# Another order of the loading phase, and of batch 4's input, in a block of two cross attentions and a gated feed-forward

## The chip, the cores and the metric

The kernel runs on one core of one Trainium2 chip. The metric is the time of one execution in microseconds (us). Engines are named as the profile names them: PE is TensorE (matrix products; PEld its weight loads), DVE is VectorE, ACT is ScalarE, POOL is GpSimd, and SP is SyncE, which here only issues transfers.

## The reference

There are 8 batches of 8 heads. x has 512 rows of 64 per head, the state 32 rows of 64. Two softmax attentions cross x and the state, and a gated feed-forward follows.

```python
scores = scale * np.matmul(x, state.transpose(0, 1, 3, 2))       # 512 x 32 per head
a = softmax(scores);   xread = np.matmul(a, state)
scores2 = scale * np.matmul(state, x.transpose(0, 1, 3, 2))      # 32 x 512 per head
a2 = softmax(scores2); sread = np.matmul(a2, x)
y = np.concatenate([xread, sread], axis=2)                       # heads side by side: (8*544, 512)
out = (1/(1+np.exp(-(y @ w_gate))) * (y @ w_val)) @ w_out        # 512 -> 1536 -> 512
```

## The kernel before

The rows of xread of one batch are worked on together, 512 at a time; the rows of sread of all batches form a last group, which the code calls batch 8 (B). The feed-forward of batches 0 and 1 is mixed into the loading phase, and batches 2 to 8 follow in a loop.

Because xread is attention times state, the kernel never forms it. It multiplies the state with the gate and value weights first (SW, the "visits" at line 231: `sw_visit` in the loading phase, `sw_wide` in the loop) and the transposed attention aT with that. Per batch the work on TensorE is:

- the scores of x with the state (`S_mm`, line 121), in two halves i = 0 and 1 of four heads each; then maximum (`S_max`) and subtraction (`S_sub`) on DVE, the exponential (`S_exp`) on ACT, sum and reciprocal (`n_sum`) on DVE and the normalising product (`n_mul`, line 152) on POOL or DVE;
- the transposed attention aT: by TensorE (`aT_mm`, copied by `aT_cp`) for batches 0 and 1, by four DMA transposes on SP (`aT_dma`, line 173) for the others;
- twelve gate-and-value products `gv_mm(b, f)` (line 283), f being a block of 128 of the 1536 hidden columns; then a tanh on ACT (`gv_th`) and one operation on DVE (`gv_glu`, line 298);
- twelve groups of four products with w_out (`out_mm`, line 314), whose results leave by SP in four stores;
- the scores of the state with x (`cT_mm` to `cT_nrm`), transposed by two DMA transposes on SP (`c_dma`, line 209), and their sums over x (`sr_mm`, line 216).

x comes in by `load_x`, is cast to bf16 (`cast_x`, line 91), and transposed: by TensorE and a copy (`xT_mm`, `xT_cp`) for batches 0 and 1, and by four DMA transposes on SP (`at_xT_dma`, line 113) for the others. The state comes in through `load_s` and `load_sb`, and `sT_mm` with `sT_pad`, `sT_cp` and `pad` lay it out transposed in sTz and sTc. `load_w` and `load_wo` fetch the weights in pieces on POOL's queue. `gate` is a tiny copy on POOL that makes what POOL issues next wait for a given tile. `warm` issues products that nobody reads.

The schedule is manual: every engine runs its instructions in the order in which the program issues them, and each waits only for what it needs. Until line 690 that order is a flat list written out call by call; this is the loading phase. PSUM has two buffers for gate products (GV), four that weight visits and others share (SWP), and one each called OU and AT; a product waits until the buffer that it is given has been read. In SBUF x has three buffers in float32, xT, aT and the attention two each.

In the loop over b from 2, block f of batch b goes with `out_mm(b - 1, f)`, and the work of the next batch nb = b + 1 is spread over the f: `row` (scores to aT_dma, in six steps t), `col` (scores of the state with x, to c_dma), the weight visits at f = 0 and 6, and x of the batch after it: loaded at f = 6, cast on POOL and transposed at f = 1. For b = 2 the steps of `row` come one f later than for the other batches, and the sums over x come at f = 9 in place of f = 3.

Of the kernel before, what the change touches and what calls it, by code (L numbers as in the profile page):

```python
# [16 lines left out]
def kernel(  # L17
# [70 lines left out]
    def cast_x(b, cp, lo, n):  # L88
        if b not in xbs:
            xbs[b] = xp.tile((128, 4, H, D), BF, name="xb" if b > 1 else "xb01", bufs=3 if b > 1 else 2)  # L90
        cp(xbs[b].rearrange("p c h d -> p h c d")[:, lo:lo + n], xfs[b][:, lo:lo + n])  # L91
# [15 lines left out]
    def xT_cp(b, j, cp):  # L107
        cp(xT_tile(b)[:, j], held["xT", b, j])
# [235 lines left out]
    def warm(n, place):  # L344

        ps = place[0].tile((128, 512), FP, name="warm", tag=place[1])
        for _ in range(n):
            nc.tensor.matmul(ps[:, :128], ones[:, 0], ones[:, 0], start=True, stop=True)  # L348
# [80 lines left out]
        nc.vector.memset(ones[:, e, 64 - e * 64:128 - e * 64], 0.0)  # L429
# [2 lines left out]
    nc.vector.memset(sTz, 0.0)
# [18 lines left out]
    xT_cp(1, 1, act)
    xT_mm(1, 2, GV)
    cast_x(1, pool, 6, 2)
    cast_x(0, vec, 0, 2)
# [3 lines left out]
    xT_mm(0, 0, AT)
    xT_mm(1, 3, SWP)
    cast_x(0, act, 2, 2)  # L460
    xT_mm(0, 1, GV)
    xT_cp(0, 0, act)
    xT_cp(1, 3, act)
    warm(3, OU)
    load_w(0, 0, 256)
# [28 lines left out]
    n_sum(1, 1)
    sT_cp(1, act)
    sw_cp(0, 256, 2, 0, act)
    warm(8, GV)
    S_max(0, 0)
    sw_visit(1, 256, 256)
# [2 lines left out]
    sw_cp(1, 256, 2, 1, act)
    S_sub(0, 0)
    S_max(0, 1)
    S_exp(0, 0)
    n_mul(1, 1, nc.gpsimd)
    aT_mm(1, GV)
# [10 lines left out]
    warm(15, GV)
    load_w(1, 1024, 512)
    gate(xfs[0][:, 7, 0, 0:1])  # L520
    aT_cp(1, 1, vec)
    gv_mm(1, 3, GV)
# [23 lines left out]
    sw_visit(1, 512, 512, 0)
    sw_visit(0, 512, 512, 0)
    gv_th(1, 1)
    sw_cp(1, 512, 0, 1, act)
    gv_glu(1, 1)  # L550
    gv_mm(0, 0, GV)
    gv_th(0, 0)
    sw_cp(0, 512, 0, 0, act)
    sw_cp(0, 512, 0, 1, vec)
# [4 lines left out]
    gv_mm(1, 4, SWP)
    gv_glu(0, 0)  # L560
    gv_mm(1, 5, GV)
    gv_th(1, 5)
    cast_x(2, vec, 4, 4)
    gv_th(1, 4)
    gv_mm(0, 2, SWP)
    gv_th(0, 2)
# [1 line left out]
    gv_glu(1, 5)
    gv_mm(0, 1, GV)
    sT_cp(3, act)  # L570
    gv_glu(1, 4)
    pad(2, 6)
    gv_glu(0, 2)
    gv_mm(0, 5, SWP)
    gv_th(0, 1)
    gv_glu(0, 1)
    sw_visit(0, 1024, 512, 0)
    gv_th(0, 5)
    gv_glu(0, 5)
    sw_cp(0, 1024, 0, 0, act)  # L580
    gv_mm(1, 0, GV)
    gate(glus[1][:, 4, 0:1])
    sw_cp(0, 1024, 0, 1, vec)
    gv_mm(0, 7, SWP)
    load_wo(0)
    sw_visit(0, 1024, 512, 1)
    gv_th(1, 0)
    gv_glu(1, 0)
    gv_th(0, 7)
    gv_glu(0, 7)  # L590
    gv_mm(0, 6, GV)
    gv_mm(0, 4, SWP)
    sw_cp(0, 1024, 1, 1, act)
    sw_cp(0, 1024, 1, 0, vec)
    gv_mm(0, 10, SWP)
    gv_mm(0, 9, SWP)
    at_xT_dma(2)
    S_mm(2, 0, SWP)
    gv_mm(0, 11, GV)
    gv_th(0, 4)  # L600
    gv_mm(0, 8, SWP)
    gv_glu(0, 4)
    out_mm(0, 0, GV)
    load_wo(1)
    gv_th(0, 6)
    gv_glu(0, 6)
# [3 lines left out]
    gv_th(0, 9)  # L610
    gv_glu(0, 9)
    gv_th(0, 11)
    gv_th(0, 8)
    load_wo(2)
# [3 lines left out]
    S_mm(2, 1, GV)
    out_mm(0, 6, AT)
    load_x(3, nc.gpsimd)  # L620
    cast_x(3, pool, 4, 4)
# [45 lines left out]
    sw_cp(1, 1024, 1, 1, vec)
    sw_cp(2, 1, 0, 0, act)
    gv_mm(1, 6, GV)
    sw_cp(1, 1024, 1, 0, act)  # L670
    cT_nrm(2, 0, nc.gpsimd)
    sw_cp(2, 1, 0, 1, act)
    gv_th(1, 6)
    gv_mm(1, 9, SWP)
    gv_th(1, 9)
    at_xT_dma(3)
    gv_glu(1, 6)
    out_mm(0, 5)
    gv_glu(1, 9)
    gv_mm(1, 8, GV)  # L680
    gv_th(1, 8)
    gv_glu(1, 8)
    gv_mm(1, 10, SWP)
    gv_th(1, 10)
    gv_mm(1, 11, GV)
    gv_glu(1, 10)
    gv_th(1, 11)
# [1 line left out]
    load_x(4, nc.sync)
    gv_glu(1, 11)  # L690
# [83 lines left out]
```

## Time and profile before

| what | value |
|---|---|
| median of 3 runs | 236.31 us (235.29 to 237.57) |
| profiled execution | 237.39 us, of which 235.6 us is the span from its first to its last instruction |
| mean granted clock of TensorE | 0.993 |
| TensorE, ACT, DVE, POOL busy | 224.3, 144.0, 139.6, 68.5 us |
| read from and written to HBM | 18.35 and 8.91 MB |

In a profile an instruction's line says when it starts, how long it takes, its engine, its source line, what it writes and reads, and in brackets how long its engine stood idle before it and what ended that. The granted clock is the share of full speed that TensorE was allowed. A transfer shows up twice: as the instruction that issues it (SPq is SP's queue) and, in the list of issues, with its time from issue to landing. Times within the span count from its first instruction.

### The profile page before, as it was taken

How to read it: one execution, taken by the hardware profiler on the slowest of the kernel's cores; microseconds unless marked ns; L12 is line 12 of the kernel's file. 1: busy time of each engine (PE TensorE's matmuls, PEld its weight loads, DVE VectorE, ACT ScalarE, POOL GpSimd, SP SyncE). 2: the span in 40 equal slices, each digit the busy share in tenths (PEclk: the TensorE clock that was granted, in tenths of full speed). 3: DMA queues.
4: the chain of work that ended last, by engine and by line, in shares of the span. 5: the costliest groups of instructions: out<-in, count | busy, mean ns of one | idle time of the engine just before them, and what ended most of it. 6: DMA issues, size and time to landing. Idle time of an engine off the chain costs nothing.

```text
span 235.6 us, 4975 instructions
## 1 busy us (share of the span) xinstructions
PE 224.3 (95%) x1887; PEld 112.4 (48%) x1887; DVE 139.6 (59%) x267; ACT 144.0 (61%) x290; POOL 68.5 (29%) x74
## 2 busy tenths in 40 slices
PE   5798999999999959999999999999999999999994
PEld 4674434444444424444444444444444444566754
DVE  3599889946586526754774567556765664432211
ACT  3679777957585825848485857585748555432311
POOL 4876180062024143303520261113110426100001
PEclk9999999999999979999999999999999999999999
DMA  6999969817553458527451665214122312311104
GB/s 205 273 200 289 180 99 188 236 36 200 127 177 67 136 138 220 156 49 268 83 143 37 178 167 123 69 56 92 46 70 67 90 57 79 89 45 67 69 22 114
DMA packets 47271, 29.49 MB, mean 125 GB/s; under 512 B 29872, under 2 KB 42544, under 8 KB 47248
## 3 DMA queue, kind: packets, MB, share of 16 engines
q1 hardware_dynamic: 40096, 21.84, 34.0%
q0 software_dynamic: 6864, 7.14, 16.4%
q10 hardware_dynamic: 288, 0.20, 0.5%
q8 instruction: 15, 0.25, 0.5%
q14 instruction: 8, 0.07, 0.1%
HBM read 18.35 MB, written 8.91 MB: 116 GB/s over the span
## 4 chain that ended last, share of the span: by engine, by line
PE 79%; DVE 6%; ACT 4%; DMA 3%; SPq 3%; issue 2%; POOL 2%; ACTq 0%; DVEq 0%; POOLq 0%
PE outp L314 33%; PE gvp L283 30%; PE gvp L286 5%; PE swp L231 4%; DVE glu L298 3%; DMA xf<-in_x_dram 2%; SPq L173 2%; ACT th L293 2%; PE Sp L121 2%; PE srp L216 1%; PE warm L348 1%; DVE rs L144 1%; PE outp L334 1%; PE cTp L181 1%; DMA aT<-ab 1%
## 5 line engine op out<-in xcount | busy, mean ns | idle before, releaser
L298 DVE SCALAR_TENSOR_TENSOR glu<-th,gvp 128x512 bf16<-128x512 f32 (+1 forms) x108 | 70.2, 657 | 72.2 <-ACT th L293 52.1
L283 PE MATMUL gvp<-aT,SW 128*128 128x512 bf16 x384 | 97.5, 379 | 3.3 <-DMA aT<-ab 2.5
L314 PE MATMUL outp<-wo,glu 128*128 128x512 bf16 x396 | 100.4, 384 | 0.0
L293 ACT ACTIVATE th<-gvp 128x512 f32<-128x512 f32 (+1 forms) x108 | 61.4, 575 | 56.2 <-PE gvp L283 46.7
L283 PEld LDWEIGHTS <-SW 128*128 128x128 bf16 x384 | 36.3, 98 | 49.3 <-issue 8.9
L314 PEld LDWEIGHTS <-glu 128*128 128x128 bf16 x396 | 37.1, 98 | 41.3 <-issue 3.4
L269 ACT CAST SW<-swp 128x512 bf16<-128x512 f32 x74 | 41.1, 587 | 4.0 <-PE swp L231 2.9
L204 POOL TENSOR_SCALAR cN<-cE,rc 128x512 bf16<-128x512 f32 x16 | 25.0, 1565 | 59.1 <-DVE rc L201 57.4
L318 ACT ACTIVATE res<-outp 128x512 f32<-128x512 f32 x33 | 19.7, 597 | 17.2 <-PE outp L314 17.0
L152 POOL TENSOR_TENSOR ab<-E,ri 128x512 bf16<-128x512 f32 x14 | 14.6, 1048 | 32.1 <-ACT E L137 15.3
L91 POOL CAST xb<-xf 128x1024 bf16<-128x1024 f32 (+1 forms) x13 | 12.5, 977 | 33.1 <-DMA xf<-in_x_dram 27.8
L269 DVE CAST SW<-swp 128x512 bf16<-128x512 f32 x22 | 14.7, 681 | 3.6 <-PE swp L231 3.6
L196 ACT ACTIVATE cE<-cTp,nb 128x512 f32<-128x512 f32 x16 | 11.1, 693 | 1.2 <-POOL cN L204 1.2
L129 DVE TENSOR_REDUCE mx<-Sp 128x16 f32<-128x512 f32 x16 | 10.9, 679 | 1.1 <-PE Sp L121 1.1
L134 DVE TENSOR_TENSOR E<-Sp,mx 128x512 f32<-128x512 f32 x16 | 11.0, 686 | 0.2
L188 DVE TENSOR_REDUCE cm<-cTp 128x1 f32<-128x512 f32 x16 | 10.9, 683 | 0.0
L144 DVE TENSOR_REDUCE rs<-E 128x16 f32<-128x512 f32 x16 | 10.8, 678 | 0.1
L137 ACT ACTIVATE E<-E 128x512 f32<-128x512 f32 x16 | 10.2, 639 | 0.5 <-DVE E L134 0.5
L325 POOL DMA_DIRECT2D out_dram<-res x2 | 1.1, 554 | 29.7 <-ACT res L318 29.7
L231 PE MATMUL swp<-wg,sTc 64*32 64x512 bf16 (+1 forms) x192 | 8.4, 328 | 0.1
L121 PEld LDWEIGHTS <-xT 128*128 128x128 bf16 x128 | 6.8, 108 | 3.2 <-issue 0.8
L231 PEld LDWEIGHTS <-sTc 64*32 64x32 bf16 x384 | 4.6, 91 | 7.4 <-issue 5.1
(62 smaller groups left out, 140.3 us busy)
## 6 DMA issues: line engine op xcount, KB each, us to landing
out_dram<-res SPq DMA_DIRECT2D x31, 256.0 KB, 2.4
xf<-in_x_dram SPq DMA_DIRECT2D x12, 256.0 KB, 4.6
xf<-in_x_dram SPq DMA_DIRECT2D x3, 1024.0 KB, 6.1
wo<-in_moe_w_out_dram POOLq DMA_DIRECT2D x3, 512.0 KB, 8.0
wv<-in_moe_w_val_dram POOLq DMA_DIRECT2D x2, 512.0 KB, 10.1
wg<-in_moe_w_gate_dram POOLq DMA_DIRECT2D x2, 512.0 KB, 9.8
xf<-in_x_dram POOLq DMA_DIRECT2D x2, 512.0 KB, 7.8
xf<-in_x_dram POOLq DMA_DIRECT2D x1, 1024.0 KB, 13.4
```

Source lines behind the costliest of these rows:

```text
L91: cp(xbs[b].rearrange("p c h d -> p h c d")[:, lo:lo + n], xfs[b][:, lo:lo + n])
L144: nc.vector.tensor_reduce(rs, halfE(b, i), AX.X, ALU.add)
L152: eng.tensor_tensor(abs_[b].rearrange("p c e (j n) -> p (c e) j n", n=Ns)[:, ce, 2 * i:2 * i + 2], halfE(b, i)[:, ce], ri[:, ce].unsqueeze ...
L204: eng.tensor_scalar(held["cN", b][:, e], held["cE", b, e], rc, None, op0=ALU.mult)
L231: nc.tensor.matmul(pss[e][j * Ns:(j + 1) * Ns, o:o + n], sTc[rows, b, j] if b > 1 else sTz[rows, b, j, e], (wg, wv)[w][rows, j, lo:lo + n] ...
L269: cp(*sw_left.pop((b, lo, w, e)))
L283: nc.tensor.matmul(ps, SWs[b][:, g, w, fs], aTs[b][:, :, g], start=(g == 0), stop=(g == 1))
L286: nc.tensor.matmul(ps, (wg, wv)[w][:, j, fs], XS[:, j], start=(j == 0), stop=(j == 3))
L293: nc.scalar.activation(th, held["gv", b, f][0], AF.Tanh, scale=0.5)
L298: nc.vector.scalar_tensor_tensor(glus[b][:, f], held["th", b, f], 1.0, held["gv", b, f][1], ALU.add, ALU.mult)
L314: nc.tensor.matmul(ops[b, c], glus[b][:, f, c * 128:(c + 1) * 128], wo[:, f], start=(f == 0), stop=(f == NF - 1))
L318: nc.scalar.activation(res, ops[b, c], AF.Copy, scale=0.5)
```

## The change

The diff leaves every helper as it is. It does three things.

The flat list of the loading phase is given another order: the first list below shows its old beginning, the second its new one up to the first gate products of batch 0. Warm-up products come first (12, 16, 3 and 3 of them, then 15); the clearing of sTz moves from the head of DVE's list to behind a cast; batch 1's two halves of scores, maxima, subtractions and exponentials follow one another directly; the first quarters of the weights are loaded first, the state of batches 4 and 5 (`load_sb(2)`) later; gate products start with f = 1, 2 and 0 of batch 1, and four of them (f = 8 to 11) wait until the end of the list.

```diff
-    nc.vector.memset(sTz, 0.0)
     load_x(1, nc.sync, 4)
-    warm(16, GV)
-    nc.scalar.activation(pre[:, 0:1], ones[:, 0, 0:1], AF.Exp)
-    cast_x(1, act, 2, 2)
-    cast_s(0, pool)
-    sT_mm(0, OU)
-    sT_pad(0, 1, vec)
-    load_x(0, nc.sync, 4)
-    cast_x(1, pool, 0, 2)
-    xT_mm(1, 0, SWP)
-    xT_cp(1, 0, vec)
...
-    S_mm(1, 0, SWP)
-    xT_cp(1, 2, vec)
-    S_max(1, 0)
...
-    S_mm(1, 1, SWP)
-    S_exp(1, 0)
...
-    S_max(1, 1)
-    xT_cp(0, 2, act)
-    load_sb(3)
-    load_w(1, 0, 256)
-    warm(6, OU)
-    S_sub(1, 1)
-    load_sb(2)
-    load_w(0, 512, 512)
```

```diff
+    warm(12, SWP)
+    warm(16, GV)
+    warm(3, SWP)
     load_x(1, nc.sync, 4)
+    warm(3, AT)
     cast_x(1, pool, 0, 2)
     xT_mm(1, 0, SWP)
+    load_w(1, 0, 256)
+    warm(15, OU)
+    nc.scalar.activation(pre[:, 0:1], ones[:, 0, 0:1], AF.Exp)
+    cast_s(0, pool)
+    load_sb(1)
+    load_w(0, 0, 256)
+    cast_x(1, vec, 4, 2)
+    nc.vector.memset(sTz, 0.0)
+    sT_mm(0, SWP)
+    load_x(0, nc.sync, 4)
+    cast_x(1, act, 2, 2)
     xT_cp(1, 0, vec)
+    xT_mm(1, 2, AT)
+    xT_mm(1, 1, GV)
+    cast_x(1, act, 6, 2)
+    sT_pad(0, 1, vec)
+    load_w(0, 256, 256)
+    xT_mm(1, 3, SWP)
     load_w(1, 256, 256)
...
+    S_mm(1, 0, GV)
+    S_max(1, 0)
+    xT_cp(1, 3, act)
+    S_mm(1, 1, GV)
+    S_max(1, 1)
...
+    S_sub(1, 1)
...
     load_w(1, 512, 512)
...
     S_sub(1, 0)
+    gate(xfs[0][:, 7, 0, 0:1])
...
+    load_sb(3)
+    load_w(0, 512, 512)
     S_mm(0, 0, GV, (0,))
+    S_mm(0, 0, AT, (1,))
+    S_exp(1, 1)
+    n_sum(1, 1)
     S_exp(1, 0)
+    sw_visit(0, 0, 256)
+    n_sum(1, 0)
+    sw_visit(1, 0, 256)
...
+    n_mul(1, 1, nc.gpsimd)
+    sw_cp(1, 0, 2, 0, act)
+    S_max(0, 0)
+    S_sub(0, 0)
+    n_mul(1, 0, nc.gpsimd)
+    aT_mm(1, AT)
+    sw_visit(1, 256, 256)
     load_sb(2)
...
+    gv_mm(1, 1, GV)
+    warm(6, SWP)
...
+    gv_mm(1, 2, SWP)
...
+    sw_visit(1, 512, 512, 1)
+    gv_mm(1, 0, GV)
...
+    sw_visit(1, 512, 512, 0)
...
+    sT_mm(2, AT)
...
+    aT_mm(0, OU)
```

At the end of the list the load of x 4 moves from behind the second transposes of batch 2 to ahead of them (`at_xT_dma(3)`, `load_x(4, nc.sync)`, ..., `c_dma(2)`). The two `n_mul` of batch 2 go from DVE to POOL; of the casts of x 2 the second half goes from DVE to POOL, and of x 3 from POOL to DVE.

In the loop, batch 3 takes the form that batch 2 has (rows one f later, sums over x at f = 9), and at b = 2 the casts and transposes of x 4 move from f = 1 to f = 6, the load of x 5 from f = 6 to f = 8:

```diff
-                if f == (4 if b > 2 else 10):
+                if f == (4 if b > 3 else 10):
                     sr_cp(b, 0, act)
                     sr_cp(b, 1, vec)
-                if 0 <= f - (b == 2) < 6:
-                    row(nb, f - (b == 2))
+                if 0 <= f - (b < 4) < 6:
+                    row(nb, f - (b < 4))
                 elif f >= 7:
                     col(nb, f - 7)
-                if f == 6 and nb + 2 < B:
+                if f == (6 if b > 2 else 8) and nb + 2 < B:
                     load_x(nb + 2, nc.sync, 4 if nb + 3 == B else 1)
-                if f == 1 and nb + 1 < B:
+                if f == (1 if b > 2 else 6) and nb + 1 < B:
                     cast_x(nb + 1, pool, 0, 4)
                     cast_x(nb + 1, pool, 4, 4)
                     at_xT_dma(nb + 1)
-            if b < B and f == (3 if b > 2 else 9):
-                sr_mm(b, AT if b > 2 else SWP)
+            if b < B and f == (3 if b > 3 else 9):
+                sr_mm(b, AT if b > 3 else SWP)
```

More of the change, by code (lines that the diff above doesn't have):

```diff
@@ L451 @@
[L451 to L454, printed above, removed]
-    S_mm(1, 0, SWP)
-    xT_cp(1, 2, vec)
-    S_max(1, 0)
[L458 to L465, printed above, removed]
-    S_sub(1, 0)
-    xT_cp(0, 1, act)
-    cast_x(0, act, 4, 2)
+    xT_cp(1, 2, vec)
+    cast_x(0, vec, 0, 2)
+    cast_x(0, pool, 4, 2)
+    xT_cp(1, 1, act)
+    S_mm(1, 0, GV)
@@ L469 @@
+    S_max(1, 0)
+    xT_cp(1, 3, act)
+    S_mm(1, 1, GV)
+    S_max(1, 1)
+    cast_x(0, act, 2, 2)
+    xT_mm(0, 1, OU)
+    xT_mm(0, 2, AT)
+    xT_cp(0, 1, act)
+    S_sub(1, 1)
+    xT_mm(0, 0, OU)
+    xT_cp(0, 2, act)
+    load_w(1, 512, 512)
+    cast_x(0, pool, 6, 2)
+    S_sub(1, 0)
+    gate(xfs[0][:, 7, 0, 0:1])
+    xT_cp(0, 0, vec)
+    xT_mm(0, 3, GV)
+    warm(8, SWP)
+    load_sb(3)
+    load_w(0, 512, 512)
     S_mm(0, 0, GV, (0,))
-    S_mm(1, 1, SWP)
+    S_mm(0, 0, AT, (1,))
@@ L494 @@
[L494 to L499, printed above, removed]
+    sw_visit(0, 0, 256)
+    n_sum(1, 0)
+    sw_visit(1, 0, 256)
+    xT_cp(0, 3, act)
+    sw_cp(0, 0, 2, 1, act)
+    S_mm(0, 1, GV, (0,))
+    S_mm(0, 1, OU, (1,))
+    sw_cp(0, 0, 2, 0, act)
+    n_mul(1, 1, nc.gpsimd)
[5 more added lines that the diff above has]
+    sw_visit(1, 256, 256)
+    load_sb(2)
@@ L500 @@
+    sw_cp(1, 0, 2, 1, act)
+    aT_cp(1, 0, act)
+    S_exp(0, 0)
+    S_max(0, 1)
+    sw_visit(0, 256, 256)
+    aT_cp(1, 1, vec)
+    S_sub(0, 1)
+    sw_cp(0, 256, 2, 0, vec)
+    sT_mm(1, OU)
+    gv_mm(1, 1, GV)
+    warm(6, SWP)
+    n_sum(0, 0)
     sw_cp(1, 256, 2, 0, act)
+    sw_cp(1, 256, 2, 1, act)
+    gv_mm(1, 2, SWP)
+    S_exp(0, 1)
     sw_cp(0, 256, 2, 1, vec)
[L502 to L507, printed above, removed]
@@ L508 @@
-    aT_cp(1, 0, act)
     load_x(2, nc.gpsimd, 2)
+    gv_th(1, 1)
     sw_visit(1, 512, 512, 1)
-    S_sub(0, 1)
-    S_exp(0, 1)
+    gv_mm(1, 0, GV)
+    gv_th(1, 2)
+    gv_glu(1, 1)
+    sT_cp(1, vec)
+    sT_mm(3, OU)
+    sw_cp(1, 512, 1, 1, act)
+    n_sum(0, 1)
+    sw_visit(1, 512, 512, 0)
+    sw_cp(1, 512, 1, 0, act)
+    gv_th(1, 0)
+    sw_visit(0, 512, 512, 0)
+    sT_cp(3, act)
+    gv_glu(1, 2)
+    load_w(0, 1024, 512)
+    n_mul(0, 0, nc.gpsimd)
+    sT_mm(2, AT)
+    load_w(1, 1024, 512)
@@ L513 @@
+    sw_cp(1, 512, 0, 1, act)
+    sw_cp(0, 512, 0, 0, act)
+    n_mul(0, 1, nc.gpsimd)
+    aT_mm(0, OU)
+    sw_cp(1, 512, 0, 0, vec)
+    aT_cp(0, 0, act)
+    aT_cp(0, 1, act)
+    gv_mm(1, 6, SWP)
+    cast_x(2, pool, 0, 4)
     sw_visit(0, 512, 512, 1)
-    sw_cp(0, 512, 1, 0, act)
-    sw_cp(1, 512, 1, 1, act)
-    load_w(0, 1024, 512)
+    gv_th(1, 6)
     sw_cp(0, 512, 1, 1, act)
[L518 to L522, printed above, removed]
@@ L546 @@
[L546 to L554, printed above, removed]
+    gv_mm(1, 5, GV)
+    gv_th(1, 5)
+    sw_cp(0, 512, 0, 1, vec)
+    gv_glu(1, 0)
+    gv_mm(0, 0, SWP)
+    gv_th(0, 0)
+    gv_glu(1, 6)
+    cast_x(2, pool, 4, 4)
+    sw_cp(0, 512, 1, 0, vec)
+    gv_glu(0, 0)
+    gv_mm(0, 5, SWP)
+    gv_mm(1, 4, SWP)
+    gv_th(1, 4)
@@ new lines @@
+    gv_mm(0, 2, GV)
+    gv_th(0, 5)
+    gv_th(0, 2)
+    gv_glu(1, 5)
+    gv_mm(0, 7, SWP)
+    gv_glu(1, 4)
+    sT_cp(2, act)
+    gv_mm(0, 6, SWP)
+    gv_th(0, 7)
+    gv_glu(0, 5)
+    gv_th(0, 6)
+    gv_glu(0, 2)
+    gv_mm(1, 7, GV)
+    gv_glu(0, 7)
+    gv_th(1, 7)
+    sw_visit(0, 1024, 512, 0)
+    sw_cp(0, 1024, 0, 0, act)
+    gv_glu(0, 6)
+    sw_cp(0, 1024, 0, 1, act)
+    sw_visit(0, 1024, 512, 1)
+    gv_glu(1, 7)
+    sw_cp(0, 1024, 1, 1, act)
+    sw_cp(0, 1024, 1, 0, vec)
@@ L555 @@
+    gv_mm(0, 4, GV)
+    pad(2, 6)
+    gv_th(0, 4)
+    load_wo(0)
+    gv_mm(0, 1, SWP)
+    gv_th(0, 1)
+    gv_mm(0, 8, SWP)
+    at_xT_dma(2)
+    gv_th(0, 8)
+    gv_mm(0, 9, GV)
+    S_mm(2, 1, OU)
+    gv_glu(0, 4)
+    gv_th(0, 9)
+    load_wo(1)
+    gv_glu(0, 1)
+    gv_glu(0, 8)
+    load_wo(2)
+    gate(glus[1][:, 4, 0:1])
+    gv_glu(0, 9)
+    S_max(2, 1)
+    gv_mm(1, 3, SWP)
+    gv_th(1, 3)
     gv_mm(0, 3, SWP)
     gv_th(0, 3)
-    cast_x(2, pool, 0, 4)
-    sw_cp(1, 512, 0, 0, vec)
@@ L559 @@
[L559 to L566, printed above, removed]
-    gv_glu(0, 3)
[L568 to L606, printed above, removed]
+    gv_glu(1, 3)
+    S_sub(2, 1)
@@ L607 @@
+    load_x(3, nc.gpsimd)
+    gv_glu(0, 3)
+    gv_mm(0, 11, SWP)
+    gv_th(0, 11)
+    gv_glu(0, 11)
+    gv_mm(0, 10, GV)
     gv_th(0, 10)
@@ L609 @@
     sw_wide(2, 0)
[L610 to L614, printed above, removed]
+    S_exp(2, 1)
+    out_mm(0, 1, GV)
+    sw_cp(2, 0, 1, 0, act)
+    sw_cp(2, 0, 2, 0, act)
+    sw_cp(2, 0, 0, 1, vec)
+    n_sum(2, 1)
+    n_mul(2, 1, nc.gpsimd)
+    sw_cp(2, 0, 2, 1, act)
+    S_mm(2, 0, SWP)
     S_max(2, 0)
+    out_mm(0, 6, GV)
+    out_mm(0, 3)
     S_sub(2, 0)
     S_exp(2, 0)
[L618 to L621, printed above, removed]
@@ L667 @@
[L667 to L687, printed above, removed]
+    n_sum(2, 0)
+    out_mm(0, 7, AT)
+    sw_cp(2, 0, 1, 1, act)
@@ new lines @@
+    out_mm(0, 5)
+    n_mul(2, 0, nc.gpsimd)
+    gate(xTs[2][:, 0, 3, 0:1])
+    aT_dma(2)
+    cast_x(3, pool, 0, 4)
+    cT_mm(2, (SWP, SWP))
+    cT_max(2, 1)
+    cast_x(3, vec, 4, 4)
+    sw_visit(1, 1024, 512, 1)
+    sw_cp(1, 1024, 1, 1, act)
+    sw_cp(1, 1024, 1, 0, act)
+    out_mm(0, 8)
+    out_mm(0, 9)
+    cT_exp(2, 1)
+    sw_visit(1, 1024, 512, 0)
+    sw_cp(1, 1024, 0, 1, vec)
+    sw_cp(1, 1024, 0, 0, act)
+    out_mm(0, 0, GV)
+    sw_cp(2, 0, 0, 0, vec)
+    out_mm(0, 11)
+    gv_mm(1, 8, SWP)
@@ new lines @@
+    gv_th(1, 8)
+    cT_max(2, 0)
+    cT_exp(2, 0)
+    gv_glu(1, 8)
+    out_mm(0, 2)
+    sw_wide(2, 1)
+    sw_cp(2, 1, 0, 0, vec)
+    sw_cp(2, 1, 1, 1, vec)
+    at_xT_dma(3)
+    load_x(4, nc.sync)
+    sw_cp(2, 1, 1, 0, act)
+    sw_cp(2, 1, 0, 1, act)
+    out_mm(0, 10)
+    gv_mm(1, 9, SWP)
+    sw_cp(2, 1, 2, 0, act)
+    gv_th(1, 9)
+    gv_glu(1, 9)
+    out_mm(0, 4)
+    gv_mm(1, 11, SWP)
+    gv_th(1, 11)
+    sw_cp(2, 1, 2, 1, vec)
+    gv_glu(1, 11)
+    gv_mm(1, 10, GV)
+    gv_th(1, 10)
@@ L688 @@
+    gv_glu(1, 10)
+    cT_nrm(2, 0, nc.gpsimd)
+    cT_nrm(2, 1, nc.gpsimd)
     c_dma(2)
[L689 to L690 removed]
     for b in range(2, B + 1):
```

81 lines of the change are left out of this document (removed).

## The prediction

> **What bounds the kernel now.** I read the page first (who is busy), then busy time by stage (where TensorE stops), then the waits of TensorE, then the queues behind the longest of them.
>
> ```profile
> PE 224.3 (95%) x1887; PEld 112.4 (48%) x1887; DVE 139.6 (59%) x267; ACT 144.0 (61%) x290; POOL 68.5 (29%) x74
> ```
>
> TensorE works 95% of the span. The next view cuts the span at the weight products that open a batch; its columns are length, then busy time (and instructions) of PE, PEld, DVE, ACT and POOL, granted clock, DMA share, GB/s.
>
> ```profile
> 0.00:10.00 10.00, 5.74 (x56) 4.65 (x57) 3.84 (x11) 4.46 (x9) 6.78 (x16) 1.00 0.90 247
> 10.00:14.30 4.30, 4.30 (x51) 4.30 (x50) 3.69 (x7) 3.66 (x8) 2.29 (x4) 1.00 1.33 202
> 14.30:24.70 10.40, 9.63 (x183) 5.13 (x180) 8.99 (x18) 8.55 (x18) 7.78 (x10) 1.00 1.26 250
> 24.70:57.70 33.00, 33.00 (x260) 14.20 (x252) 25.89 (x46) 24.70 (x48) 10.30 (x12) 1.00 0.77 157
> 57.70:81.70 24.00, 23.92 (x201) 11.04 (x200) 15.67 (x29) 16.36 (x34) 4.04 (x4) 1.00 0.49 129
> 81.70:110.20 28.50, 25.86 (x209) 11.62 (x216) 15.68 (x29) 16.68 (x34) 7.77 (x7) 0.94 0.56 152
> 110.20:134.30 24.10, 23.98 (x208) 10.89 (x212) 15.59 (x29) 16.43 (x34) 7.16 (x7) 1.00 0.46 120
> 134.30:158.50 24.20, 24.08 (x209) 10.99 (x216) 15.60 (x29) 16.53 (x34) 7.26 (x7) 1.00 0.43 113
> ```
>
> From 24.7 us TensorE has no gap for 33 us, and batch after batch takes 24.0 to 24.2 us. One stage doesn't fit: the stage of batch 3 (81.7 to 110.2) takes 28.5. The waits of TensorE, and two cuts inside that stage, say why:
>
> ```profile
> PE gvp L283 <- DMA aT<-ab: 2.5, 1, 2.5
> 82.60:85.10 2.50, 0.01 (x1) 0.04 (x2) 0.25 (x2) 0.67 (x2) 2.25 (x2) 1.00 0.25 51
> 86.00:89.50 3.50, 3.50 (x17) 1.53 (x16) 1.98 (x3) 0.31 (x1) 0.00 (x0) 0.51 0.87 285
> ```
>
> The first gate product of batch 3 waits 2.5 us for the transposed attention (aT) of batch 3, and behind that stop the granted clock is 0.51 for 3.5 us, another 3.5 x 0.49 = 1.7 us. Together 4.2; the stage is 28.5 - 24.1 = 4.4 too long. I take 4.3. Why aT is late stands in the lists of POOL, DVE, SP and TensorE and in the chain:
>
> ```profile
> 63.20 0.57 SPq L74 DMA_DIRECT2D xf<-in_x_dram  x1
> 69.40 2.02 POOL L91 CAST xb<-xf 128x1024 bf16<-128x1024 f32 x2 [14.38 <-DMA xf<-in_x_dram]
> 71.39 2.06 POOL L152 TENSOR_TENSOR ab<-E,ri 128x512 bf16<-128x512 f32 x2
> 71.36 0.25 DVE L146 RECIPROCAL ri<-rs 128x16 f32<-128x16 f32 x1
> 71.45 5.13 SPq L113 DMA_TRANSPOSE xT<-xb  x4
> 77.78 6.04 SPq L173 DMA_TRANSPOSE aT<-ab  x4
> 82.58 2.38 DMA aT<-ab
> 83.93 0.52 SPq L74 DMA_DIRECT2D xf<-in_x_dram  x1
> 61.95 0.40 PE L121 MATMUL Sp<-sTz,xT 128*128 128x64 bf16 x8
> ```
>
> x of batch 4 is asked for at 63.20 and lands about 69.4. POOL's casts of it hold it to 71.4, so batch 3's normalisation (L152) ends at 73.45. SP's four transposes of x (5.13 us), then two output stores, stand ahead of aT, which starts at 77.78 although its data was there at 73.45; its last piece lands at 84.96. TensorE wanted it at about 82.5. So aT is 4.3 us late by the queue's order and 2.5 us late for its reader.
>
> **The change part by part.** *Stage of batch 2.* The casts and transposes of x of batch 4 go from f = 1 to f = 6, behind batch 3's aT; the load of x 4 goes ahead of batch 2's second transposes (c_dma), that of x 5 from f = 6 to f = 8. The last row sum of batch 3 is ready at 71.36 + 0.25 = 71.6. With no cast ahead, POOL's second product starts there and ends at 72.7 (half of 2.06 each). aT starts then, takes 6.04 with its last issue 4.8 us in (77.78 to 82.58), and lands 2.38 later: 79.9, against 82.5. The wait goes, and with it the low clock: -4.3. Bounds: none of the low clock returned, -2.5; all of the stage's excess, -4.4.
>
> The Trainium skill ("TensorE: Matmul & The Clock Gate", Part 1) has the clock fall after an idle window of about 3.4 us, free-running; by that a stop of 2.5 us need not cost clock, and the term would be -2.5 and the whole 234.9. The 0.51 row disagrees here, and the row decides.
>
> What is late next? x 4's transposes follow aT: 78.8 to 83.9, last piece landing some 2.4 us after its issue, 85.1. Batch 4's first scores now sit at f = 1 of batch 3; batch 2's stage has that form today, and there they start 61.95 - 57.7 = 4.25 into it: 85.95. Margin 0.8. The load of x 5 follows at about 84.4 (store at f = 8 between); such loads land in
>
> ```profile
> xf<-in_x_dram SPq DMA_DIRECT2D x3, 1024.0 KB, 6.1
> ```
>
> 6.1 us: 90.5. Casts 2.0 and transposes 5.1 end at 97.7, two stores 1.0, so aT of batch 4 starts at 98.7 and lands 7.2 later at 105.9; TensorE wants it at 81.7 + 24.1 + 0.8 = 106.6. Margin 0.7: I put 0.2 for this, between 0 and, if x 5 came as late in its stage as x 4 does today, the same 4.3 again. The second transposes, pushed behind x 4 and x 5, feed the sums over x (sr_mm); those of batch 3 move to f = 9 with the score rows, where batch 2's are today; no cost.
>
> *Loading phase.* The same loads, casts, copies and products in another order. Two of POOL's products of batch 2 replace DVE's, one cast of x 2 goes to POOL and one of x 3 to DVE. TensorE fills its gaps there with warm-up products, so what counts is when the in-order chain on DVE lets it go. Rows that carry the chain (DVE unless another engine is named):
>
> ```profile
> xf<-in_x_dram SPq DMA_DIRECT2D x2, 256.0 KB, 4.4
> 8.16 0.61 DVE L91 CAST xb<-xf 128x512 bf16<-128x512 f32 x1 [2.12 <-DMA xf<-in_x_dram]
> 1.24 0.91 DVE L432 MEMSET sTz<- 128x1024 uint32 x1 [0.16 <-issue]
> 5.62 0.42 DVE L108 COPY xT<-xTp 128x512 bf16<-128x512 bf16 x1 [0.62 <-PE xTp L105]
> L129 DVE TENSOR_REDUCE mx<-Sp 128x16 f32<-128x512 f32 x16 | 10.9, 679 | 1.1 <-PE Sp L121 1.1
> L134 DVE TENSOR_TENSOR E<-Sp,mx 128x512 f32<-128x512 f32 x16 | 11.0, 686 | 0.2
> L144 DVE TENSOR_REDUCE rs<-E 128x16 f32<-128x512 f32 x16 | 10.8, 678 | 0.1
> L269 ACT CAST SW<-swp 128x512 bf16<-128x512 f32 x74 | 41.1, 587 | 4.0 <-PE swp L231 2.9
> 13.73 2.05 POOL L152 TENSOR_TENSOR ab<-E,ri 128x512 bf16<-128x512 f32 x2 [1.25 <-DVE ri L146]
> 18.97 1.02 PE L283 MATMUL gvp<-aT,SW 128*128 128x512 bf16 x4
> 22.73 0.62 PE L159 MATMUL aTp<-ident,ab 128*128 128x128 bf16 x8 [0.48 <-POOL ab L152]
> ```
>
> The third part of x 1 is issued near 1.8 and lands 4.4 later: 6.2. DVE casts it (6.8), and only then clears sTz, which today is done by 2.15: 0.91 (7.7). Two copies and a pad of 0.42 (8.9), a cast (9.4). Both maxima and both subtractions of batch 1, waiting until 9.6 for scores that follow a pad and two copies on ACT (an estimate): 4 x 0.68 = 12.3. A copy, then two sums with reciprocals of 0.97: ready at 13.7 and 14.65, so POOL's two products end at 15.75. Today they end at 13.73 + 2.05 = 15.78. Taking both halves first gains nothing, because the late clear eats it. Then maximum, subtraction, maximum for batch 0 (16.7); aT's copy on DVE follows ACT's, which stands behind four weight copies (14.7 + 5 x 0.59 = 17.6), and ends at 18.0; the last subtraction frees the PSUM buffer of the first gate product's second half at 18.7. So that product is done near 19.2 (today 18.97 + 1.02 = 20.0). But DVE has weight copies, sums and glu in front of it still: 18.7 + two copies 1.3 + sum 0.95 + glu 0.65 + small copy 0.35 + sum 0.95 + glu 0.65 = 23.5, when the product of weights at line 231 gets its PSUM buffer; with it, its twin and sT, aT of batch 0 starts at 24.5, against 22.73. At 25.1 TensorE then has three gate products and seven weight visits behind it; today, at 24.7, three and eight, and a visit takes 0.4. Loss 0.8, and 0.1 for short waits on glu up to 31 us: +0.9. Bounds: the first gate product's lead, -0.8; and 24.5 - 22.73 plus two 0.4 visits out of place, +2.6.
>
> From there to the loop all gate products of batch 0 and 1 but four come before the outputs. DVE is busy 25.9 of 33.0 us there and ACT 24.7, with no stop on TensorE, and the change leaves both engines' number of instructions as it is to within two; cost 0. x 4, at present landing at 69.4, then comes near 65.
>
> Sum: -4.3 + 0.2 + 0.9 = -3.2. The profiled execution took 237.39 (span 235.6 and 1.79 around it), so 234.2; it is 1.08 above the median of the runs, 236.31, so 233.1 on the median's scale, which I forecast. A measurement of this kernel tells about 1% from no change (runs of 235.29 to 237.57), 2.4 us.
>
> **The rivals.** *The full clock comes early (232.3).* The pace of the warm-up products changes today:
>
> ```profile
> 1.02 1.89 PE L348 MATMUL warm<-ones 128*128 128x128 bf16 x16 [1.02 <-DVE ones L429]
> 13.08 1.42 PE L348 MATMUL warm<-ones 128*128 128x128 bf16 x12
> 17.85 1.01 PE L348 MATMUL warm<-ones 128*128 128x128 bf16 x15
> ```
>
> 118 ns each until 14, 67 after, and only once TensorE had been busy without a break from 10 us. After, 34 such products run back to back (34 x 0.118 = 4.0 us), so it could be fast from 5 us, and transposes, scores and visits up to 18 take half their time: the 0.8 comes back. For it: the dense start. Against: gaps between 7 and 13, and DVE, not TensorE, times this phase. That is what the skill's warm-up rule on the same page (about 3.4 us of sustained work) would make of it; the pace rows agree with it.
>
> *The wait moves to batch 4 (237.4).* Were x 5 to land 3 us later in its stage than 90.5, aT of batch 4 would miss its reader by 2.5 and the clock would fall: 233.1 + 4.3. For it: a margin of 0.7 only. Against: x 5 is now asked for 26.7 us into the stage of batch 2, three us earlier for its use than x 4 today.
>
> *The loading phase costs 1.7 more (234.8),* its upper bound: every buffer wait falls on TensorE.
>
> *Slower: the state of batches 4 and 5 comes late (239.7).* load_sb(2) moves on POOL from 10.37 to behind batch 1's products, 15.8. Its transposes stand on TensorE ahead of aT of batch 0 and everything after.
>
> ```profile
> 10.37 0.60 POOL L359 DMA_DIRECT2D sb<-in_state_dram  x1
> sb<-in_state_dram POOLq DMA_DIRECT2D x3, 64.0 KB, 8.4
> xf<-in_x_dram POOLq DMA_DIRECT2D x1, 1024.0 KB, 13.4
> ```
>
> At 8.4 it lands at 24.2, just in time for 24.3. At 13.4, POOL's slowest, it lands at 29.2: 4.9 of stop and 1.7 of clock, 233.1 + 6.6. Over 1% slower from a landing at 28.0. Against: it is small, and only weights issued before it are ahead of it.
>
> **How the numbers follow.** Forecast 0.50; early clock 0.20; loading at its bound 0.10; wait moved 0.12; late state 0.08. Faster by over 1% is below 233.9: early clock, and 0.48 of the forecast's 0.50: 0.68. Slower (over 238.7): 0.08. The rest, 0.24, is within 1%. Range: from 230.8 (the loading bound of -0.8 in place of +0.9, and 0.6 for the spread of runs) to 236.5, which leaves out the moved wait and the late state.
>
> **What would show it.** Right: no wait of L283 on aT, clock 1.0 at 80 to 90, the stage of batch 3 near 24.2 us, aT of batch 3 issued near 73 after the opening of batch 2 at about 58; aT of batch 0 near 24.5. Wrong: a stop of L283 a batch later, a wait of L369 on the state's DMA, or gaps between 25 and 57 us.

## The result and the profile after

The kernel after takes 234.56 us (median of 20 runs, 232.84 to 235.91) against 236.62 (20 runs, 234.72 to 238.33): 0.9908 of before, 95% interval 0.9884 to 0.9932. That is 2.1 us or 0.9%, a gain, but under 1%; 233.1 was forecast. The traced execution took 233.25 us with a span of 231.5. Its page, and its stages cut at the opening of each batch (the first weight product of `sw_wide`), with the columns explained ahead of the prediction's second view:

```profile
PE 221.3 (96%) x1887; PEld 110.6 (48%) x1887; DVE 138.2 (60%) x266; ACT 143.0 (62%) x288; POOL 71.6 (31%) x77
```

```profile
24.70:56.50 31.80, 31.80 (x260) 13.80 (x253) 24.20 (x41) 23.54 (x46) 9.87 (x13) 1.00 0.83 156
56.50:80.50 24.00, 23.92 (x203) 11.04 (x202) 15.83 (x31) 16.35 (x34) 7.17 (x6) 1.00 0.62 132
80.50:104.50 24.00, 23.92 (x201) 11.03 (x200) 15.60 (x29) 16.41 (x34) 7.22 (x6) 1.00 0.60 141
104.50:129.90 25.40, 24.24 (x201) 10.87 (x201) 15.59 (x29) 16.56 (x34) 7.66 (x7) 1.00 0.64 161
129.90:154.00 24.10, 23.98 (x201) 10.92 (x200) 15.58 (x29) 16.42 (x34) 7.16 (x7) 1.00 0.40 107
```

The rows are the end of the loading phase and the stages of batches 2, 3, 4 and 5. The stage of batch 3 is down from 28.4 to 24.0, with the clock at 1.00. That of batch 4, regular before, is 1.3 too long. The waits of TensorE and SP's list show why:

```profile
PE gvp L283 <- DMA aT<-ab: 0.6, 1, 0.6
PE srp L216 <- DMA Eb<-cN: 0.4, 1, 0.4
```

```profile
58.24 0.58 SPq L74 DMA_DIRECT2D xf<-in_x_dram  x1
71.67 5.04 SPq L173 DMA_TRANSPOSE aT<-ab  x4
76.81 6.46 SPq L113 DMA_TRANSPOSE xT<-xb  x4
84.01 0.39 SPq L74 DMA_DIRECT2D xf<-in_x_dram  x1
92.66 5.57 SPq L113 DMA_TRANSPOSE xT<-xb  x4
99.43 5.06 SPq L173 DMA_TRANSPOSE aT<-ab  x4
104.60 0.52 SPq L74 DMA_DIRECT2D xf<-in_x_dram  x1
106.53 3.01 SPq L209 DMA_TRANSPOSE Eb<-cN  x2
```

Read it downwards. Batch 3's aT goes out at 71.67, ahead of x 4's transposes, as the change says. Behind those, x 5 is asked for at 84.01; its transposes start at 92.66, aT of batch 4 only at 99.43, and the first gate product of batch 4 waits 0.6. x 6 then goes out at 104.60, 1.9 us ahead of the second transposes of batch 4 (Eb), for which the sums over x wait another 0.4. The stop that the change removes has come back one stage later, smaller, and without the loss of clock.

### The profile page after: what moved, and what is told of

Read it like the earlier page. It is cut to its first block, busy times and chain, and to the rows that moved or that the text cites. A ratio compares the mean times of both kernels' runs of the same rounds, so it can differ in the third digit from the quotient of the medians.

```text
span 231.5 us, 4984 instructions
## 1 busy us (share of the span) xinstructions
PE 221.3 (96%) x1887; PEld 110.6 (48%) x1887; DVE 138.2 (60%) x266; ACT 143.0 (62%) x288; POOL 71.6 (31%) x77
## 3 DMA queue, kind: packets, MB, share of 16 engines
q0 software_dynamic: 6864, 7.14, 16.7%
## 4 chain that ended last, share of the span: by engine, by line
PE 79%; DVE 7%; DMA 4%; ACT 4%; POOL 2%; issue 2%; SPq 1%; ACTq 0%; DVEq 0%; POOLq 0%
PE outp L314 33%; PE gvp L283 31%; PE gvp L286 5%; PE swp L231 4%; DVE glu L298 3%; DMA Eb<-cN 2%; DMA xf<-in_x_dram 2%; PE srp L216 2%; POOL cN L204 1%; PE cTp L181 1%; ACT th L293 1%; PE outp L334 1%; PE Sp L121 1%; DVE rs L144 1%; ACT SW L269 1%
## 5 line engine op out<-in xcount | busy, mean ns | idle before, releaser
L314 PE MATMUL outp<-wo,glu 128*128 128x512 bf16 x396 | 99.0, 379 | 0.0
L283 PE MATMUL gvp<-aT,SW 128*128 128x512 bf16 x384 | 97.4, 379 | 1.5 <-DMA aT<-ab 0.6
L283 PEld LDWEIGHTS <-SW 128*128 128x128 bf16 x384 | 36.3, 98 | 47.0 <-issue 6.2
L314 PEld LDWEIGHTS <-glu 128*128 128x128 bf16 x396 | 36.6, 98 | 40.7 <-issue 2.8
L204 POOL TENSOR_SCALAR cN<-cE,rc 128x512 bf16<-128x512 f32 x16 | 24.9, 1564 | 64.5 <-DVE rc L201 55.7
L152 POOL TENSOR_TENSOR ab<-E,ri 128x512 bf16<-128x512 f32 x16 | 16.7, 1047 | 42.5 <-DVE ri L146 34.8
L91 POOL CAST xb<-xf 128x1024 bf16<-128x1024 f32 (+1 forms) x14 | 13.6, 987 | 15.0 <-PE gvp L283 6.6
L121 PEld LDWEIGHTS <-xT 128*128 128x128 bf16 x128 | 6.0, 100 | 4.4 <-issue 1.0
```

The lines of the kernel that those rows point to most:

```text
L152: eng.tensor_tensor(abs_[b].rearrange("p c e (j n) -> p (c e) j n", n=Ns)[:, ce, 2 * i:2 * i + 2], halfE(b, i)[:, ce], ri[:, ce].unsqueeze ...
L204: eng.tensor_scalar(held["cN", b][:, e], held["cE", b, e], rc, None, op0=ALU.mult)
L283: nc.tensor.matmul(ps, SWs[b][:, g, w, fs], aTs[b][:, :, g], start=(g == 0), stop=(g == 1))
L314: nc.tensor.matmul(ops[b, c], glus[b][:, f, c * 128:(c + 1) * 128], wo[:, f], start=(f == 0), stop=(f == NF - 1))
```

## The experiments

Two theories stood against each other after the result. A, the prediction's: the stop came from the order, x 4's casts and transposes ahead of batch 3's attention. B: it came from x 4 being asked for too late, and the list's move of that load is what counts. The table gives, from each trace, the opening of batch 2 and the lengths of the stages of batches 3 and 4 (starts of the first weight products), and the ratio to before.

| kernel | opening of batch 2 | stage 3 | stage 4 | median us | ratio, 95% interval |
|---|---|---|---|---|---|
| before | 57.7 | 28.4 | 24.1 | 236.62 | 1 |
| after | 56.5 | 24.0 | 25.4 | 234.56 | 0.9908 (0.9884 to 0.9932) |
| after, second trace | 57.2 | 24.0 | 25.7 | 234.01 | 0.9891 (0.9858 to 0.9924) |
| loop alone | 57.0 | 24.0 | 25.9 | 234.11 | 0.9900 (0.9867 to 0.9932) |
| list alone | 56.5 | 24.1 | 24.1 | 232.22 | 0.9818 (0.9784 to 0.9851) |
| before, x 4 sooner | 56.3 | 24.9 | 24.1 | 232.56 | 0.9822 (0.9788 to 0.9856) |
| list alone, x 4 late | 57.0 | 29.2 | 24.1 | 237.10 | 1.0028 (0.9993 to 1.0064) |
| after, x 5 at f = 6 | 57.0 | 26.3 | 24.1 | 234.35 | 0.9889 (0.9858 to 0.9921) |
| after, x 5 at f = 3 | 56.8 | 24.0 | 24.1 | 232.18 | 0.9814 (0.9783 to 0.9845) |
| list and row shift | 56.8 | 24.0 | 24.1 | 232.30 | 0.9810 (0.9777 to 0.9844) |
| x 4 sooner and row shift | 57.1 | 24.0 | 24.1 | 232.41 | 0.9857 (0.9813 to 0.9901) |
| list alone, clear first | 56.7 | 24.3 | 24.1 | 232.30 | 0.9802 (0.9769 to 0.9834) |
| list alone, few warm-ups | 56.5 | 24.7 | 24.1 | 232.30 | 0.9822 (0.9789 to 0.9855) |

**The loop alone.** The list of before with the loop of after.

```diff
-                if f == 6 and nb + 2 < B:
+                if f == (6 if b > 2 else 8) and nb + 2 < B:
...
-                if f == 1 and nb + 1 < B:
+                if f == (1 if b > 2 else 6) and nb + 1 < B:
```

> The list of the loading phase as before, the loop as after: casts and transposes of x 4 at f = 6 of batch 2's stage, x 5 loaded at f = 8, batch 3 in batch 2's form. Theory A (the prediction's: the stop in the stage of batch 3 came from x 4's casts and transposes standing ahead of batch 3's attention): the loading phase ends at 57.7 as before, the stage of batch 3 takes 24.0 to 24.2 in place of 28.5, the stage of batch 4 about 1.3 more (x 5 late, as in the trace of after), ratio near 0.987. Theory B (the stop came from x 4 being asked for too late; the list's earlier load is what removes it): the same stage times, since this order doesn't need x 4 early. Theory C (the profiled run of before shows a longer stop than a typical one): ratio 0.992 to 0.996 although the profile shows the whole 4 us gone.

Stage 3 is whole again, stage 4 is 1.8 too long, ratio 0.990: the loop brings the change's whole gain, and its whole loss, without the new list. The ratio lies between the 0.987 of theories A and B and the 0.992 of C; the section on the prediction comes back to C.

**The list alone.** The list of after with the loop of before: x 4 is still cast at f = 1, ahead of batch 3's attention.

> The list as after, with x 4 loaded ahead of the second transposes of batch 2, the loop as before: casts and transposes of x 4 at f = 1, ahead of batch 3's attention on POOL and SP. Theory A: the order is what counts, the stop of L283 on aT in the stage of batch 3 stays (1 to 2.5 us, with a low clock behind it), ratio 0.995 to 1.004. Theory B: x 4 is asked for at 58.2, lands near 64.6, its casts end at 66.7 and its transposes on SP at 72, so aT of batch 3 starts at 72 to 73 and lands by 80, ahead of its reader at 81.3: no stop, and none in the stage of batch 4 either, since x 5 is asked for at f = 6; ratio 0.976 to 0.983, faster than the whole change.

```profile
58.04 0.58 SPq L74 DMA_DIRECT2D xf<-in_x_dram  x1
66.64 5.14 SPq L113 DMA_TRANSPOSE xT<-xb  x4
72.98 5.05 SPq L173 DMA_TRANSPOSE aT<-ab  x4
```

SP's list of this run: x 4's transposes do stand ahead of aT, and do no harm, because x 4 landed at 64.6 and they are through when the attention is ready. No wait of TensorE in stages 3 and 4, and 0.982, twice the gain of the whole change. Theory A's order is sufficient, as the loop alone showed, but not needed; B stands.

**One line.** Before, with the load of x 4 moved as in the change.

```diff
     at_xT_dma(3)
+    load_x(4, nc.sync)
     gv_glu(1, 6)
...
     c_dma(2)
-    load_x(4, nc.sync)
```

> The kernel before with one line moved: x 4 is loaded behind the transposes of x 3 and ahead of the second transposes of batch 2. Theory A: the casts and transposes of x 4 still stand ahead of batch 3's attention, so most of the stop stays: 1.5 us or more, ratio 0.995 to 1.0. Theory B: x 4 is issued near 60.5 in place of 63.2 and lands near 66.6, everything behind it comes 2.7 us sooner, aT of batch 3 lands near 82.2 against a reader at 82.5: stop 0 to 0.5, no low clock, stage of batch 3 24.1 to 24.8, ratio 0.982 to 0.988.

0.982 again. The 0.8 too much in stage 3 is a wait of 0.6 of the sums over x for batch 3's second transposes, which now come to stand close behind the load of x 5 (81.93 against 78.29); the row shift below takes it away by asking for them later. The run with few warm-ups has the same wait, of 0.4, with the new list (stage 3 of 24.7), so it belongs to neither list.

**The list without that line.**

> The list as after, but x 4 loaded at its very end, behind the second transposes of batch 2, as before; the loop as before. Theory B (the stop hangs on when x 4 is asked for, and on nothing else in the list): x 4 issued near 63, landed near 69, aT of batch 3 issued near 77.5 against a reader near 81.5, a stop of about 2 to 2.7 us with half clock behind it, ratio 0.996 to 1.003. Rival (something else in the new order of the list, such as batch 2's products on POOL, takes the stop away): no stop, ratio 0.981 to 0.984.

```profile
62.59 0.57 SPq L74 DMA_DIRECT2D xf<-in_x_dram  x1
71.04 5.13 SPq L113 DMA_TRANSPOSE xT<-xb  x4
77.37 6.56 SPq L173 DMA_TRANSPOSE aT<-ab  x4
```

```profile
PE gvp L283 <- DMA aT<-ab: 3.4, 1, 3.4
84.50:88.00 3.50, 2.80 (x7) 1.02 (x8) 0.83 (x2) 0.60 (x1) 0.00 (x0) 0.57 0.67 169
```

SP's list, the wait, and the window that follows it: with x 4 asked for at 62.59 the stop is back, 3.4 us, and the granted clock is 0.57 behind it. So of the long reordered list one line carries the time. The ratio is 1.0028: nothing else in it is worth anything that this run can tell, though its stop is also 0.9 us longer than that of before.

**The second trace of after.**

> The kernel after, unchanged: a second trace of it. Its first trace is 4.1 us shorter than that of before, the medians differ by 2.1. Theory C (executions differ in where TensorE's clock is low): loading phase or the stop in the stage of batch 4 longer by 1 us or more in this trace, with half clock where it is. Theory D (they don't; the two first traces were ends of a spread without a place): stages within 0.3 us of the first trace of after. Ratio 0.991 by either.

Opening 0.7 later than in the first trace, stage 4 25.7: the executions do differ, mostly in the loading phase, but by less than a microsecond and at full clock in stage 4, so neither theory holds as it stood. The 0.7 is there from the start: DVE's cast of the third part of x 1 begins when that part has landed, at 6.59 in place of 5.80, and all that follows is late by as much.

**Where the 1.3 to 1.8 us of stage 4 come from.** Undone first: the load of x 5 at f = 8, back to f = 6 (ahead of x 4's transposes on SP).

> The kernel after with one number undone: x 5 is loaded at f = 6 of batch 2's stage as before, on SP ahead of the transposes of x 4 in place of behind them. Theory E (the 1.3 to 1.8 us that the change loses in the stage of batch 4 come from x 5 alone: late x 5, late transposes of it, late aT of batch 4, late x 6 and with it the late second transposes of batch 4): x 5 issued near 77 and landed near 84, aT of batch 4 issued near 96 in place of 99.4 to 100, no wait on aT or Eb in the stage of batch 4, which takes 24.1 to 24.4; ratio near 0.983. Theory F (it comes from batch 3's rows standing one f later): the stage of batch 4 still 0.8 us or more too long; ratio 0.987 to 0.991.

```profile
77.34 0.52 SPq L74 DMA_DIRECT2D xf<-in_x_dram  x1
77.96 5.50 SPq L113 DMA_TRANSPOSE xT<-xb  x4
xT<-xb SPq DMA_TRANSPOSE x4, 6.9
PE Sp L121 <- DMA xT<-xb: 1.5, 4, 0.8
```

Theory E was right about stage 4, which is regular, and missed on the ratio: stage 3 is now 2.2 too long. The third row is the list of issues for 77.9 to 83.5: each transpose of x 4 lands 6.9 us after its issue, in the list alone 2.5. The 1 MB load issued right ahead of them, which lands 6.2 us after its issue, is still on its way, and batch 4's scores wait in four pieces. So x 5's load has no good place beside x 4's transposes; the next run puts it well ahead of them.

```diff
-                if f == (6 if b > 2 else 8) and nb + 2 < B:
+                if f == (6 if b > 2 else 3) and nb + 2 < B:
```

> The kernel after with x 5 loaded at f = 3 of batch 2's stage: behind nothing on SP, before batch 3's aT is issued, and landed before the transposes of x 4 start; casts and transposes of x 4 still at f = 6. Theory G (what the change loses again is the place of x 5's load alone: behind the transposes it comes too late, right ahead of them it slows them): x 5 issued near 64 to 66 and landed before 73, transposes of x 4 landing 2.5 to 3.2 us after issue, no wait of TensorE on a transfer in the stages of batches 3 and 4, both 24.0 to 24.2; ratio 0.979 to 0.984. Theory H (casting and transposing x 4 behind batch 3's attention loses it in itself): one of the two stages 0.7 us or more too long, ratio 0.985 to 0.991.

```profile
64.48 0.39 SPq L74 DMA_DIRECT2D xf<-in_x_dram  x1
71.98 5.04 SPq L173 DMA_TRANSPOSE aT<-ab  x4
77.11 6.08 SPq L113 DMA_TRANSPOSE xT<-xb  x4
xT<-xb SPq DMA_TRANSPOSE x4, 3.1
```

x 5 leaves in SP's pause at 64.48, the transposes land in 3.1, stages 3 and 4 are 24.0 and 24.1 with no wait of TensorE, ratio 0.981. Theory G holds: transposing x 4 behind batch 3's attention costs nothing in itself; the place of x 5's load cost what the change lost.

**The row shift.** Batch 3's rows one f later and its sums over x at f = 9, first with the new list, then with the old list and x 4 sooner.

> The list as after and x of batches 4 and 5 as before (cast at f = 1, loaded at f = 6); of the loop's change only batch 3's rows one f later with the sums over x at f = 9. Theory E: nothing is lost by that; stage of batch 4 24.1 to 24.4, ratio 0.981 to 0.984 as with the list alone. Theory F: the stage of batch 4 has the wait on the second transposes (0.4 us or more), ratio 0.985 to 0.990.

> The kernel before with x 4 loaded ahead of the second transposes of batch 2, and batch 3's rows one f later with its sums over x at f = 9; casts and transposes of x 4 at f = 1, load of x 5 at f = 6, list otherwise as before. If the loading order is worth nothing, ratio 0.979 to 0.983 as with the new list and the same loop, no wait on aT or Eb, stages of batches 3 and 4 24.0 to 24.3; if the new list is worth 0.5 us or more, 0.983 to 0.986.

Both traces have stages of 24.0 and 24.1 and no wait on a transfer in them: the shift loses nothing, theory F falls. The two medians differ by 0.1 us, though the lists differ. The second ratio, 0.986, lies in the range put down for a list that is worth 0.5 us or more, but its interval, 0.981 to 0.990, separates nothing: the runs of before beside it ranged from 234.11 to 240.06.

**Inside the loading phase.** The clear of sTz back at the head of DVE's list, and 16 warm-ups in place of 34 at the start, each on the list alone.

> The list as after and the loop as before, with the clearing of sTz put back at the head of DVE's list. The prediction's step (the late clear, 0.91 us on DVE, holds up batch 1's scores and all that follows): scores, maxima and products of batch 1 come 0.5 to 0.9 sooner, the first gate product near 16.4 in place of 17.2, the opening of batch 2 0.5 to 0.9 sooner than 56.5; ratio 0.978 to 0.980. Rival (TensorE waits there for other things: the casts of x on ACT, POOL's products, the weights): no more than 0.2 sooner, ratio 0.981 to 0.983.

> The list as after and the loop as before, with 16 warm-up products at the start in place of 34. The rival of the early clock (the dense start opens TensorE's clock by about 5 us and with it shortens the loading phase): products at half pace (about 107 ns a product of 128 columns) from 5 to 12 us, the first gate product 0.5 us or more later than 17.2, opening of batch 2 57.0 to 57.6, ratio 0.984 to 0.986. The prediction's reading (DVE times this phase, the clock changes little): opening within 0.3 of 56.5, ratio 0.981 to 0.983.

DVE and TensorE with the clear first, then TensorE with few warm-ups, then the same stretch of after, with the granted clock that follows:

```profile
6.65 0.77 DVE L91 CAST xb<-xf 128x512 bf16<-128x512 f32 x1 [4.50 <-DMA xf<-in_x_dram]
9.47 1.29 DVE L129 TENSOR_REDUCE mx<-Sp 128x16 f32<-128x512 f32 x2 [0.47 <-PE Sp L121]
15.56 0.62 PE L159 MATMUL aTp<-ident,ab 128*128 128x128 bf16 x8 [1.39 <-POOL ab L152]
16.96 0.30 PE L231 MATMUL swp<-wv,sTz 64*32 64x256 bf16 x8 [0.55 <-DMA wv<-in_moe_w_val_dram]
22.40 0.63 PE L231 MATMUL swp<-wg,sTz 64*32 64x512 bf16 x16 [0.63 <-DMA wg<-in_moe_w_gate_dram]
```

```profile
5.20 1.81 PE L348 MATMUL warm<-ones 128*128 128x128 bf16 x15
```

```profile
4.99 1.00 PE L348 MATMUL warm<-ones 128*128 128x128 bf16 x15
5.80 0.49 DVE L91 CAST xb<-xf 128x512 bf16<-128x512 f32 x1 [4.73 <-DMA xf<-in_x_dram]
6.45 0.91 DVE L446 MEMSET sTz<- 128x1024 uint32 x1 [0.16 <-issue]
9.36 1.29 DVE L129 TENSOR_REDUCE mx<-Sp 128x16 f32<-128x512 f32 x2 [0.40 <-PE Sp L121]
15.45 0.62 PE L159 MATMUL aTp<-ident,ab 128*128 128x128 bf16 x8 [0.91 <-POOL ab L152]
10.00:15.00 5.00, 4.10 (x72) 3.42 (x72) 4.86 (x11) 3.62 (x8) 3.95 (x7) 0.66 1.43 196
```

With the clear first, batch 1's maxima start at 9.47 in place of 9.36, which looks as if the clear had held up nothing. But in this trace the third part of x 1 landed later, so that DVE's cast of it starts at 6.65 in place of 5.80. Counted from that cast, the maxima come 2.8 us later with the clear first, and 3.5 to 3.7 us later in all eight traces with the late clear. So the late clear does cost about 0.7 us on DVE's chain, as the prediction had it. None of this shows at the opening of batch 2 (56.7), for besides the late part of x 1 TensorE waits 0.55 and 0.63 for weights here; what an early clear would be worth there stays open.

With few warm-ups the next 15 products take 1.81 us in place of 1.00, and batch 2 opens at the same 56.5. The early clock is real, but in after it is given back: the granted clock is 0.66 between 10 and 15 us, and 1.00 there with few warm-ups. Together the two buy nothing.

## Why the prediction was right, and where it was not

**Stage of batch 3, -4.3.** Measured -4.4 (28.4 to 24.0). aT was to be issued 15.0 us after the opening of batch 2 and went out 15.2 after it (71.67 less 56.49); the low clock left with the stop, as the term had it. The Trainium skill ("TensorE: Matmul & The Clock Gate", Part 1) names about 3.4 us of idling for the clock to fall, by which only 2.5 was to be had; a stop of 3.4 us did give 0.57 here, but one of 2.5 gave 0.51 just as well, and a wait of 0.6 left it at 1.00. Whether a stop of 2.5 always costs clock is another matter; see the sum below.

The reason given for the stop was half of it. The prediction had x 4's late landing and its place in the queue, and laid the 4.3 us to the order. The runs show that either cure is enough alone, and that the load, which it costed only as "then comes near 65", is the cheaper one: one line, and no loss a stage later.

**What is late next, 0.2.** The mis-sized term: 1.3 in the first trace, 1.6 in the second, 1.8 with the loop alone. Step by step: x 4's transposes took 6.46 us on SP, not 5.1, so x 5 was issued 27.5 us into the stage of batch 2, not 26.7; it landed in 6.5; its own transposes took 5.57; a margin of 0.7 became a wait of 0.6. That is the rival of the moved wait, at a small size. Not seen at all was the second half: aT of batch 4 pushed late also pushes x 6's load against the second transposes of batch 4, of which the last lands 5.65 us after its issue.

**Loading phase, +0.9.** Measured -0.2: the traces with the old list open batch 2 at 57.7, 57.0, 56.3 and 57.1, those with the new list at 56.5, 57.2, 56.5, 57.0, 56.8, 57.0 and 56.8, means 57.0 and 56.8. Traces of one list differ by more than that, so it is no gain that they can tell, but it isn't a loss of 0.9. The rows of after that carry the chain:

```profile
13.34 2.05 POOL L152 TENSOR_TENSOR ab<-E,ri 128x512 bf16<-128x512 f32 x2 [1.05 <-DVE ri L146]
14.03 2.05 ACT L269 CAST SW<-swp 128x512 bf16<-128x512 f32 x4 [0.92 <-PE swp L231]
16.11 0.59 ACT L169 COPY aT<-aTp 128x512 bf16<-128x512 bf16 x1
22.31 0.41 PE L231 MATMUL swp<-wg,sTz 64*32 64x512 bf16 x7 [0.29 <-DVE glu L298]
22.96 0.62 PE L159 MATMUL aTp<-ident,ab 128*128 128x128 bf16 x8
```

Up to POOL's two products the chain came out nearly as put down, the late clear with it: they end at 15.4, where 15.75 was put. The step that failed is what follows. ACT's copy of aT was put at 17.6 and ends at 16.7: ACT's four weight copies start at 14.0, not 14.7, and take 2.05 us, not 4 x 0.59. DVE then lets the weight products go at 22.3 in place of 23.5, and aT of batch 0 starts at 23.0 in place of 24.5. From there to the opening of batch 2 TensorE works without a stop, for 33.5 us in every trace with the new list and 35.0 in every one with the old; the numbers of the prediction come to 34.1 (57.7 + 0.9 - 24.5). So aT of batch 0 does come later with the new list, at 23.3 against 22.1 on the means, and there is 1.45 us less work behind it, which the prediction put at 0.9.

That DVE and not TensorE's clock times this phase was right for the pair of after and few warm-ups. It isn't the whole story: in three other traces of the new list (list and row shift, list alone with x 4 late, x 5 at f = 3) the low clock comes between 15 and 25 us, 0.83 on the mean, and batch 2 opens 41.3 to 41.6 us after aT of batch 1 in place of 41.0 in after. Up to 0.6 us seems to be lost in that way.

**The sum.** The first traces differ by 4.1 us, the medians by 2.1. 1.0 of this gap is chance in the loading phase: before was traced at its latest opening, after at its earliest, 1.2 apart where the means are 0.2 apart. With the means of the openings and the second trace's stage 4, the traces give 4.4 - 1.6 + 0.2 = 3.0, against 2.1 and 2.6 in the two comparisons of medians.

Most of the rest may be the clock behind the stop, which the one trace of before cannot tell. The mean clock is on record for the 49 runs of before that the ratios of the experiments rest on: 35 read 0.991 to 0.993, as the traced run does, with a median of 236.8 us, and 14 read 0.998 or more, with 235.6. The three kernels with the old list and without that stop (loop alone, x 4 sooner, x 4 sooner and row shift) read 0.998 or more in all their 21 runs. So it looks as if some three executions of before in ten had the stop and lost no clock. With 1.7 us of clock lost in the others only, the 3.0 becomes 2.5. No execution of that kind was traced, so this is argued and not shown; theory C of the first experiment would hold for a minority of the executions.

Two terms were off by over a microsecond in opposite directions, stage 4 by 1.4 and the loading phase by 1.1. That the sum of the traces, -3.0, comes so near to the -3.2 put down is luck; stage 3 is the term that was right for its reason. The numbers of the prediction nearest to the measured 234.56 are those of other cases, 234.8 for the loading phase at its bound, which did not come, and 234.9 for a stop that costs no clock, which may hold for those three in ten. Faster by over 1% had a chance of 0.68; the measured gain is 0.9%, with an interval from 0.7 to 1.2%, because stage 4 takes back a third of what stage 3 gives, where 0.2 was put. Of the signs of being wrong one came, the stop of L283 a batch later; TensorE waited nowhere for the late state, and had no gap between 25 and 57 us.

## What to carry to other kernels

Before reordering a queue around a late transfer, ask how early the first transfer of its chain could be issued: here one line, which asks for x 4 some 3 us earlier in its stage, was worth twice the reordering. When a step is moved behind another in a queue, follow what stands behind the moved step, for as many stages as the queue runs ahead, and look at what each bulk load shares the DMA engines with. Openings of stages over several traces separate a term of a microsecond from the spread, which one pair of traces does not. And before a step is said to cost nothing, count from the transfer that starts its chain: a part of x 1 that landed 0.85 us later hid the 0.7 us of the clear.
